# A written-out order of all engines, replaced by another, in a transformer block on one core

## The chip, the core and the metric

The kernel runs on one core of one Trainium2 chip. The metric is the device time of one execution in microseconds (us). A second number is the span, from the first to the last instruction of the core in a profiled execution. An engine is one of PE (TensorE, matrix products), DVE (VectorE), ACT (ScalarE), POOL (GpSimd), and SP (SyncE, which only issues transfers here). DMA stands for the transfers between the device's main memory and the on-chip memory.

## The reference

One block of a transformer, 2048 rows of 512 in fp32, one batch. The condition `c` gives six vectors by one product; attention and a feed-forward part follow, each behind a layer norm that two of the vectors scale and shift.

```python
mod = (_silu(c) @ w_mod).reshape(c.shape[0], 6, 1, -1)
sa, ca, ga, sb, cb, gb = (mod[:, i] for i in range(6))
h = _layernorm(x, axis=-1) * (1 + ca) + sa
x = x + ga * _A_ref(h, A_wq, A_wk, A_wv, A_wo, A_beta)
h = _layernorm(x, axis=-1) * (1 + cb) + sb
x = x + gb * _B_ref(h, B_w1, B_b1, B_w2, B_b2)
```

`_A_ref` has 32 heads of 16 and goes through the rows in 4 segments of 512. In each segment it takes causal softmax attention inside the segment, mixed by a gate with a read from a memory `M, z` that the earlier segments have filled (`num = phi(q) M`, `den = phi(q) z`); then the segment's keys and values are added to the memory. `_B_ref` is `relu(x @ w1 + b1)**2 @ w2 + b2` with 1792 hidden columns.

## The kernel before

The kernel has no loop that runs on the chip. Python builds a list of 3905 nodes; a node is a few instructions of one engine (`op("ACT", duration, fn, priority, after=..., get=..., put=...)`). `Plan.run` plays the nodes through a small model of the engines, hands out buffers in the order in which the model frees them, and the instructions are then emitted in the order that it found. Where the module constant `ORDER` lists an engine's nodes by number, that engine takes them in exactly that order. All five engines are listed in full, so `ORDER` is the order of each engine's queue; the model's durations decide only which buffer a node gets.

The work goes by row blocks of 512 (`s`, 0 to 3), in attention by units (`u = 4 s + cc`, a quarter of the heads each), with half units `qd`.

- **Start.** The six transfers of `w_mod`, `x`, `wq`, `wk`, `wv` are issued on SP. PE runs warm-up products (`bwarm`, nodes 8 to 77, line 536, two passes each) between its first real work. `ln_transposed` (line 621) turns one 128-row tile of the normed rows: PE transposes into `blnq` (nodes 105, 111, 117, 123 for the tiles 0 to 3 of block 0), ACT and DVE scale and shift (`lnf`, lines 611 and 613), ACT casts the high part into `HT` (line 618; nodes 108, 114, 120, 126), and DVE subtracts it to get the low part (line 618; nodes 109, 115, 121, 127; on POOL for later blocks). Every operand of an exact product is split so, into a high and a low part of the type fp32r, and a product takes three matmuls.
- **Weights.** `split_w` casts `wq`, `wk` (tile `WQK`) and `wv` (`WVO`) on ACT (line 695) and subtracts on POOL (line 699), by 128 columns: nodes 130 and 131 are the first columns of `wq`, 140 and 141 those of `wk`. The first QK products are the nodes 280 to 297 (lines 779 to 781): 280 to 283 and 290 to 293 are for the rows of the tiles 0 and 1. `clear` fills `ST` with zeros by DMA (nodes 158 to 160).
- **Attention.** For each unit: QK, split (`sg`, lines 821 and 823), twelve transfers that lay the heads out in `ST` (line 839), scores for the row maxima (`ba`, lines 894 and 899), scores again (`bpb`, line 1063), exp on ACT (`pt`, line 1080), the causal mask on POOL (line 1067), times V (`bpv`, line 1122). Meanwhile `make_w1` prepares `w1` in main memory (`w1d`) for the feed-forward part.
- **FFN.** For each row block, seven blocks of 256 hidden columns. `fetch_w1` brings one block's weights into one of two buffers (`w<-w1d`, line 1425; 3684 to 3687 are the blocks 3 to 6 of the last row block). Seven products of half blocks (`bh`, line 1475) are put together on DVE, squared, split (`rr`), and multiplied with `w2` into `bpf` (lines 1539 to 1541). When a row tile is done, DVE adds it to the rows (line 1550) and a store leaves on SP (line 1552): nodes 3122 to 3131 are the stores of row block 0, 3379 to 3388 of block 1, 3636 to 3645 of block 2, and 3893, 3896, 3899, 3902 of block 3 (3904, on ACT, is half of the last tile). Before that, the rows get the term `b2` on DVE (line 1545).

SP issues its transfers in the listed order: one that waits for its data holds up those behind it. The end of the SP list before:

```python
3681-3683 3636 3684-3685 3128 3379 3686 3125 3687
3902 3122 3645 3642 3899 3893 3896 3388 3382 3385 3639
```

Of the kernel before, what the change touches and what calls it, by code (L numbers as in the profile page):

```python
# [69 lines left out]
1160-1161 1259 1170 1497 1173 1498 1178 1401 1359 1182-1183 1407 1184 1256 1540 1275 1541 1250 1542 1278 1543 1186  # L70
1282 1545 1290 1546 1285 1547 1364 1262 1548 1373 1523-1524 1380 1367 1525 1388 1294-1296 1370 1298 1526 1391 1301
1528 1305 1376 1529-1531 1394 1308 1659-1660 1557 1661 1565 1662 1599 1313 1664-1665 1385 1602 1666-1667 1571 1397
1317 1605 1318-1319 1410 1794 1568 1795 1321 1578 1796 1413 1797 1562 2074 2079 1586 1799 1592 1800 1417 1801 1420
1574 1802 1425 1734 1692 1429 1583 1433 1430-1431 1436 1929-1930 1589 1931 1440 1932 1448 1452 1443 1934 1706 1935
1608 1936-1937 1611 1595 1453 1703 2084 1700 2089 1454 1697 1615 1713 1721 1618 1456 1623 1627 1718 1737 1628 1709
1631 1740 1638 1869 1634 1629 1724 1641 1827 1841 1646 1650 1727 1743 1872 1651-1652 1832 1746 2093 1750 1730 2094
1835 1753 2095 1848 1838 2096 1654 1758 1875 1762 1862 1766 1763-1764 1844 1773 2098 1769 2099 1776 2100 1856 1781
2101 2004 1962 1785-1787 2007 1859 2122 1853 1878 2123 1885 2124 1970 1865 2125 1888 1789 2127 1881 2128 1973 2129
1983 2130 2251 1997 2252 2198 1893 2253-2254 1976 1988 1897-1899 1967 1901 2256 1991 2257 1979 1908 2258 1916 2259
1994 2139-2140 2156 2141-2142 2170 1911 1904 2144-2146 2167 2000 2147 2177 2191 1920 2164 2013 1921-1922 2010 2161  # L80
2020 2375 2016 2376 2028 2188 2377 2173 2378 2023 1924 2380 2185 2381-2382 2301 2182 2383 2032-2034 2036 2306 2322
2499 2043 2500 2039 2501 2194 2502 2309 2051 2315 2504-2505 2280 2506 2046 2312 2507 2285 2055 2288 2201 2056-2057
2318 2204 2059 2208 2211 2291 2216 2220 2446 2224 2227 2221-2222 2231 2294 2234 2243 2641 2239 2404 2409 2244 2418
2297 2245 2644-2645 2651 2646-2647 2325 2332 2328 2654-2655 2247 2340 2335 2656 2661 2657 2415 2425 2344-2346 2412
2348 2355 2664-2665 2671 2666-2667 2421 2439 2528 2351 2674-2675 2358 2536 2363 2681 2676-2677 2430 2542 2436
2684-2687 2721 2367-2369 2449 2433 2724-2726 2691 2456 2533 2452 2727 2694-2695 2442 2371 2459 2549 2696 2731 2697
2762 2464 2539 2468-2470 2472 2563 2545 2734-2735 2701 2557 2479 2482 2736 2704-2705 2737 2560 2475 2487 2706 2741
2707 2554 2491-2493 2573 2580 2583 2744-2746 2566 2576 2495 2588 2747 2774 2711 2592-2594 2596 2603 2570 2599
2714-2715 2611 2606 2716 2770 2717 2751 2615-2617 2766 2754 2619 2755-2757 2791 2781 2811 2801 2794 2784 2804
2785-2786 2805 2787 2795 2806 2796-2797 2906 2903-2905 2814 2807 2815 2908 2907 2909 2816 2929 2926-2927 2817 2928  # L90
2930 2932 2931 3064 3068 3066-3067 2949 2952 2950-2951 3065 3070 2954 3071 2953 3069 3076 2955 2975 3134 3078 2973
2972 2974 3072 3082 3074 2976 3142 3083 2978 2977 2999 3080 2995-2998 3000 3138 3081 3087 3084-3085 3001 3086 3091
3018 3023 3088 3019 3092 3021 3020 3090 3022 3095 3146 3024 3089 3099 3041 3046 3042 3096 3093 3045 3043 3097 3044
3047 3094 3098 3391 3100 3104 3103 3102 3107-3108 3176 3106 3110 3101 3105 3178 3114 3174 3109 3175 3113 3177 3196
3179 3195 3111 3180 3115 3119 3200 3198 3197 3118 3199 3117 3399 3123 3112 3116 3201 3126 3218 3321 3129 3325 3120
3324 3217 3216 3395 3219 3328 3222 3322-3323 3238 3220 3327 3221 3237 3326 3333 3243 3339 3329 3337 3331 3239 3241
3240 3242 3335 3341 3343 3345 3403 3260 3258 3340 3264 3344 3338 3342 3259 3348 3262 3261 3347 3263 3346 3352 3351
3283 3279 3284 3281 3280 3356 3355 3282 3350 3349 3301-3302 3285 3353 3300 3354 3303 3357 3361 3305-3306 3358 3362
3304 3365 3359 3363 3431-3432 3660 3367 3360 3364 3434 3368 3372 3366 3433 3370 3435 3369 3437 3453 3652 3374 3373
3436 3380 3452 3376 3648 3458 3454 3371 3656 3375 3377 3455-3456 3383 3386 3457 3474 3473 3479 3478 3475-3477  # L100
3580-3581 3584 3579 3578 3590 3582 3494-3496 3585-3586 3497 3499 3498 3583 3500 3596 3519 3592 3515 3588 3516-3517
3594 3597 3518 3595 3521 3599 3601 3520 3605 3600 3598 3536-3537 3541 3602 3606 3604 3608-3609 3613 3540 3538-3539
3610 3603 3542 3612 3558 3607 3557 3611 3559 3614-3615 3560 3563 3619 3616 3620 3562 3561 3623 3617 3689 3688 3618
3691 3627 3690 3624 3621 3693 3628 3694 3625 3622 3692 3629 3626 3630 3711 3634 3710 3633 3631 3712 3709 3714 3643
3715 3713 3732 3730 3736 3632 3733 3637 3640 3835 3838 3731 3837 3842 3849 3841 3734 3836 3735 3847 3751 3754 3753
# [12 lines left out]
1068 1067 687 924 699 675 698 674 686 1071 783-784 199 934 936 932 929 935 931 933 930 1073-1074 780 706 779 704 707
206 714 713 941 721-722 1482 709-710 717 955 950 948-949 956 947 716 952 946 953 951 1000-1001 1195 209 809-810 801
# [277 lines left out]
def block_kernel(ctx, tc, x, wq, wk, wv, wo, beta, w1, b1, w2, b2, c, wmod, out):  # L397
# [71 lines left out]
    op = PL.op  # L469
    TL = {}  # L470
# [149 lines left out]
    def ln_transposed(s, t, src, dst, pool, sc, bi, pr, after, put, wait=(), low="DVE", kind="#D"):  # L620

        b = ("lnq", sc, s, t)
        f = ("lnf", sc, s, t)
        n = pe("F", 0.357, lambda: ln_turn(bank(b), src()), pr, after=after, get=[(kind, b)] + ([(pool, f)] if pool != "xr" else []),
               put=put)
# [5 lines left out]
        h = act(512, lambda: ln_split(dst(), t, TL[f], low)[0](), pr + 0.02, sbuf=True, after=[*af, *wait], put=[f])  # L631
# [965 lines left out]
```

## Time and profile before

| | us |
|---|---|
| three runs: median (lowest to highest) | 796.09 (795.66 to 796.46) |
| the profiled execution | 795.43 |
| its span | 793.7 |
| PE busy | 764.5 (96%) |
| DVE, ACT, POOL busy | 599.3, 441.7, 323.4 |

A row of a timeline has the start, the duration, the engine, the line, the operation, the tiles that it writes and reads, and in brackets the idle time before it and what ended that. SPq and ACTq are issues of transfers. A row of waits has who waited for whom, the time in all, how often, and the longest. A row of windows has the busy time of each engine in a stretch, with the number of instructions, then the granted PE clock (1.00 is full), the mean busy share of the DMA engines and GB/s. Matmul ends are modelled, so a busy PE isn't PE at its peak.

### The profile page before, as it was taken

The numbers are of one execution on the slowest core, as the hardware profiler recorded it, in microseconds if no ns is written. First come the engines' busy times: TensorE is split into PE (matmuls) and PEld (weight loads), VectorE is DVE, ScalarE is ACT, GpSimd is POOL, SyncE is SP. The second block draws the span as 40 slices with busy tenths as digits, with TensorE's granted clock in tenths as the row PEclk, the third lists the DMA queues.
The fourth block names the chain that finished last, engine by engine and source line by source line (L and its number), as shares of the span: only waits on it lengthen the run. The fifth ranks groups of instructions, "written<-read, shape, count | busy, mean of one in ns | idle before, by whom it ended". The sixth has DMA issues, their size and how long they took to land.

```text
span 793.7 us, 18015 instructions
## 1 busy us (share of the span) xinstructions
PE 764.5 (96%) x6649; PEld 606.7 (76%) x6649; DVE 599.3 (76%) x1591; ACT 441.7 (56%) x1001; POOL 323.4 (41%) x400
## 2 busy tenths in 40 slices
PE   9899999989999999999999999999999999999995
PEld 8777666765677656787576669898989889889984
DVE  5688758978789678989988789787866876476543
ACT  2568967789878898686865653556121321121110
POOL 4576674688777887545342252442002010000000
PEclk9999989999999999999999999999999999999998
DMA  9576856542644533435452275665543454544613
GB/s 313 138 195 171 246 181 196 160 135 94 192 128 133 169 94 96 131 86 159 130 141 81 82 252 199 213 239 199 186 169 116 180 204 181 186 165 160 233 53 145
DMA packets 59265, 129.65 MB, mean 163 GB/s; under 512 B 8613, under 2 KB 23977, under 8 KB 55594
## 3 DMA queue, kind: packets, MB, share of 16 engines
q1 hardware_dynamic: 59026, 128.37, 50.3%
q8 instruction: 53, 0.87, 0.5%
q14 instruction: 34, 0.28, 0.1%
q10 hardware_dynamic: 152, 0.13, 0.1%
HBM read 81.29 MB, written 20.19 MB: 128 GB/s over the span
## 4 chain that ended last, share of the span: by engine, by line
PE 61%; ACT 8%; DVE 4%; DMA 2%; SPq 1%; issue 1%; POOL 1%; ACTq 0%; DVEq 0%; POOLq 0%
PE bh L1475 16%; PE bpf L1540 6%; PE bpf L1539 6%; PE bpf L1541 6%; PE bpv L1122 5%; PE bqk L787 4%; PE bpb L1063 3%; PE ba L894 3%; ACT pt L1080 3%; PE bv L860 2%; PE bwop L1218 2%; PE bwop L1220 2%; PE bwop L1219 2%; ACT lnf L611 1%; SPq L839 1%
## 5 line engine op out<-in xcount | busy, mean ns | idle before, releaser
L899 DVE CUSTOM_DVE_ANT_0 ba<-ba,msk 128x512 f32<-128x512 f32 (+2 forms) x384 | 192.3, 533 | 36.9 <-PE ba L894 23.3
L1080 ACT ACTIVATE pt<-bpb 128x512 f32<-128x512 f32 x320 | 173.7, 619 | 22.4 <-PE bpb L1063 19.1
L1475 PEld LDWEIGHTS bh<-H2o,w 128*128 128x128 f32 x1176 | 153.9, 189 | 11.6 <-ACT h2raw L1281 1.4
L1475 PE MATMUL bh<-H2o,w 128*128 128x256 f32 x1176 | 157.8, 282 | 1.4 <-DVE h2raw L1283 0.8
L1067 POOL TENSOR_SCALAR_AFFINE_SELECT pt<-pt 128x512 f32<-128x512 f32 x128 | 79.6, 638 | 87.7 <-ACT pt L1080 65.0
L787 PE MATMUL bqk<-HT,WQK 64*128 64x512 f32 x720 | 104.4, 399 | 0.0
L1521 ACT CAST rr<-xx 128x512 fp32r<-128x512 f32 x56 | 34.4, 620 | 97.3 <-DVE xx L1511 60.2
L894 PE MATMUL ba<-ST 63*128 63x256 f32 (+2 forms) x512 | 79.7, 351 | 5.5 <-DMA ST<-sg 1.4
L1122 PE MATMUL bpv<-pt,VT 128*32 128x512 f32 (+3 forms) x1024 | 83.7, 448 | 0.7 <-POOL pt L1067 0.4
L1063 PE MATMUL bpb<-ST 64*128 64x256 f32 (+2 forms) x512 | 80.4, 352 | 2.2 <-ACT e L828 0.7
L787 PEld LDWEIGHTS bqk<-HT,WQK 64*128 64x128 f32 x720 | 73.3, 187 | 6.5
L894 PEld LDWEIGHTS ba<-ST 63*128 63x128 f32 x512 | 51.4, 186 | 31.2 <-ACT pt L1080 7.1
L1063 PEld LDWEIGHTS bpb<-ST 64*128 64x128 f32 x512 | 52.5, 188 | 21.1 <-ACT pt L1080 4.7
L1539 PE MATMUL bpf<-w,rr 128*128 128x512 f32 x160 | 63.5, 397 | 0.0
L1540 PE MATMUL bpf<-w,rr 128*128 128x512 f32 x160 | 63.0, 393 | 0.0
L1541 PE MATMUL bpf<-w,rr 128*128 128x512 f32 x160 | 62.5, 391 | 0.0
L860 PE MATMUL bv<-WVO,HT 64*128 64x512 f32 x384 | 54.9, 397 | 0.0
L899 DVE DVE_READ_ACCUMULATOR2_ANT mx<- 128x1 f32 x384 | 54.3, 141 | 0.0
L1122 PEld LDWEIGHTS bpv<-pt,VT 128*32 128x32 f32 x1024 | 27.3, 110 | 33.7 <-issue 25.5
L1523 DVE TENSOR_TENSOR rr<-xx,rr 128x512 fp32r<-128x512 f32 x56 | 40.0, 720 | 12.7 <-ACT rr L1521 12.6
L1501 ACT COPY p<-bh 128x256 f32<-128x256 f32 x28 | 10.4, 371 | 63.2 <-PE bh L1475 34.9
L1498 DVE SCALAR_TENSOR_TENSOR u<-bh,b1c,u 128x256 f32<-128x256 f32 x56 | 26.9, 480 | 24.3 <-PE bh L1475 23.2
(171 smaller groups left out, 1459.8 us busy)
## 6 DMA issues: line engine op xcount, KB each, us to landing
w<-w1d SPq DMA_DIRECT2D x28, 1792.0 KB
ST<-sg SPq DMA_DIRECT2D x192, 128.0 KB
w1d<-X1L SPq DMA_DIRECT2D x21, 512.0 KB
xt<-in_A_x SPq DMA_DIRECT2D x16, 256.0 KB
wm<-in_w_mod SPq DMA_DIRECT2D x16, 256.0 KB
xw<-in_A_x SPq DMA_DIRECT2D x16, 256.0 KB
X1L<-in_B_w SPq DMA_DIRECT2D x7, 512.0 KB
wr<-in_B_w SPq DMA_DIRECT2D x14, 256.0 KB
```

The costliest lines, as they stand in the source:

```text
L787: nc.tensor.matmul(bank(banks[w]), W3(w, k, x, cols.start, cols.stop)[r], HT[r, y, k], start=turn == k == i == 0, stop=turn == 1 and k == ...
L860: nc.tensor.matmul(bank(banks[t]), HT[r, x, k, (t2 + t) * P:(t2 + t + 1) * P], WVO[r, k, y], start=turn == k == i == 0, stop=turn == 1 and ...
L894: nc.tensor.matmul(dst[:, c0:c0 + n], ST[b:b + 63, 0, sl, qt * P:(qt + 1) * P], ST[b:b + 63, 1, sl, :n], start=True, stop=True)
L899: nc.vector.tensor_tensor_reduce(i, i, msk[:, 512 - n:], scale=1.0, scalar=-3e38, op0=ALU.add, op1=ALU.max, accum_out=o)
L1063: nc.tensor.matmul(dst, ST[b:b + 64, 1, sl, kb * P:(kb + 1) * P], ST[b:b + 64, 0, sl, q0:512], start=True, stop=True)
L1067: nc.gpsimd.affine_select(out=ap, in_=ap, pattern=[[0, ap.shape[1]], [1, P]], compare_op=ALU.is_ge, fill=0.0, base=0, channel_multiplier=-1)
L1080: ns = [op("ACT", 0.49, lambda j=j: nc.scalar.activation(buf("PPP"[n], pt)[:, i + j], bank(keys[j]), AF.Exp, scale=0.25), pr[slot] + 0.01 ...
L1122: nc.tensor.matmul(bank(o)[32 * hq:32 * hq + 32, q0:q0 + src.shape[1]], v[:, a:a + 32], src, start=start, stop=stop, tile_position=(0, 32 ...
L1475: nc.tensor.matmul(pb(i), A[:, x, kk], B[:, y, kk], start=kk == j == 0, stop=kk == 1 and j == 2)
L1539: nc.tensor.matmul(q, rh, wh, start=(i == 0), stop=False)
L1540: nc.tensor.matmul(q, rh, wl, start=False, stop=False)
L1541: nc.tensor.matmul(q, rl, wh, start=False, stop=(i == NF - 1))
```

## The change

All five lists of `ORDER` are replaced: the same nodes in another order. On PE 889 of 1315 nodes have another place, 212 by more than five; on ACT 742 of 945; on DVE 693 of 897; on POOL 238 of 342; on SP 331 of 403. The lists were searched for the mean end over six sets of durations, with the end of the stores counted. Beside that, the low part in `ln_transposed` is marked `lock=True`, by which the model lets it share one port with POOL's operations. The parts of the lists that the prediction speaks of:

```diff
 "PE", start
-... 3 28-40 86 94 111 41 88 42-45 96 46-51 123 52 105 53 117 54-77 280-281 290 282-284 291-292 ...
+... 3 27-37 105 38-41 111 42 86 94 43 88 96 44-47 123 48-52 117 53-72 290 73-77 280-281 291 282-284 292 ...
 "ACT", start
-1 4 87 95 112 130 124 106 118 140 126 108 120 114 150 152 142 ...
+1 4 87 95 130 140 112 124 106 114 108 126 118 120 150 142 144 ...
 "DVE", start
-2 98-99 110 101 100 89 122 97 104 113 116 125 107 119 127 109 121 115 151 ...
+2 98-99 101 104 110 100 122 89 97 113 116 125 107 119 115 109 127 121 151 ...
 "POOL", start
-102-103 141 131 143 157 133 153 155 ...
+102-103 141 131 143 133 157 155 153 ...
 "SP", start
-82 78 90 79 83-84 91 85 92-93 81 80 128 138-139 129 148-149 5 858 860-861 859 158 160 159 ...
+78-79 82 90 85 81 92 83 91 84 93 80 128 138-139 160 158 148 129 149 858-861 5 ... 161 159 ...
 "PE", around node 532 (modulation columns in attention)
-... 575-577 652 579 532 670 ...
+... 575-577 532 652 579 670 ...
 "ACT", around node 531 (its copy)
-... 896 898 657-658 902 905 531 899 ...
+... 896 898 902 899 531 657-658 905 ...
 "SP", the fills of unit 8 (1511 to 1522)
-... 1518 242 1516 1514 1513 1512 1265 1511 1522 1519-1521 246 245 1515 1517 1379 249 ...
+... 1515 1522 1517 1519 1521 242 1514 1265 1511 1516 1512 1518 1513 246 245 1379 249 1520 ...
 "PE", end
-... 3888 3886 3885 3889-3890 3894 3900 3887 3891 3897
+... 3877 3886 3883 3890 3887 3881 3885 3900 3889 3897 3891 3888 3894
 "SP", end
-3681-3683 3636 3684-3685 3128 3379 3686 3125 3687
-3902 3122 3645 3642 3899 3893 3896 3388 3382 3385 3639
+3681-3683 3385 3684 3388 3685 3645 3128 3382 3122 3379 3125 3686 3642 3636 3687 3131 3639
+3902 3899 3893 3896
@@ ln_transposed
-        l = op(low, 1.24 if low == "POOL" else 0.6, lambda: ln_split(...)[1](), pr + 0.03, after=[h], put=[f])
+        l = op(low, 1.24 if low == "POOL" else 0.6, lambda: ln_split(...)[1](), pr + 0.03, after=[h], put=[f], lock=True)
```

More of the change, by code (lines that the diff above doesn't have):

```diff
@@ new lines @@
+1331-1332 980 1333 1134 1334 992 1097 1137 1110 728 850 1118 1005 851-852 1121 1008 1012 1124 1015 854 1020 1471 1100
+1094 1476 1024 1028 1103 1115 1269 1486 1031 1025 1272 1106 1224 1232 1035 1038 1026 1238 1043 1047 1235 1140
+1048-1049 1127 1147 1490 1143 1229 1491 1051 1155 1492 1150 1493 1245 1159 1404 1253 1495 1241 1496 1163 1166
+1160-1161 1259 1170 1497 1173 1498 1178 1401 1359 1182-1183 1407 1184 1256 1540 1275 1541 1278 1542 1250 1543 1186
+1282 1545 1290 1546 1285 1364 1547 1262 1548 1373 1523 1380 1524 1367 1525 1388 1294-1296 1370 1298 1526 1391 1301
@@ new lines @@
+1835 1753 2095 1848 1838 2096 1654 1758 1875 1762 1862 1766 1763-1764 1856 1773 2098 1776 2099 1769 1844 2100 1781
+2101 2004 1962 1785-1787 1859 1878 2122 1853 2123 2007 1885 2124 1865 2125 1970 1888 1789 2127 1983 2128 1881 2129
+1973 2130 1997 2251-2252 1988 2253 1893 2198 2254 1976 1897 2010 1898-1899 1967 1901 2256 1908 2257 1916 1991 2258
+1979 2259 1994 2139 2156 2140-2142 1904 1911 2167 2144-2145 2170 2000 2146 2177 2191 2147 1920 2164 2013 1921-1922
+2188 2020 2375 2161 2376 2185 2377 2016 2378 1924 2023 2380-2381 2028 2182 2382 2173 2383 2301 2306 2032-2034 2036
@@ new lines @@
+2322 2499-2500 2043 2312 2501 2194 2502 2039 2309 2051 2504-2505 2315 2046 2506-2507 2280 2288 2055 2285 2201
+2056-2057 2318 2208 2059 2204 2211 2291 2216 2220 2224 2446 2227 2221-2222 2231 2234 2294 2641 2239 2243 2404 2418
+2297 2244-2245 2409 2644 2651 2645-2646 2325 2328 2332 2654 2647 2655 2335 2340 2415 2656 2661 2657 2425 2412
+2344-2346 2348 2355 2247 2664 2671 2665-2666 2439 2351 2421 2667 2674 2528 2536 2363 2675 2681 2676-2677 2542 2358
+2436 2684-2687 2721 2367-2369 2433 2449 2430 2724-2726 2691 2456 2533 2452 2727 2694-2695 2442 2371 2459 2549
@@ new lines @@
+2696-2697 2731 2464 2539 2563 2468-2470 2472 2545 2762 2734 2557 2479 2482 2735 2701 2736-2737 2475 2487 2560
+2704-2707 2741 2491-2493 2573 2580 2554 2583 2744-2745 2566 2576 2495 2588 2746 2711 2774 2747 2592-2594 2596 2603
+2599 2714-2715 2751 2606 2570 2611 2716-2717 2766 2615-2617 2770 2754 2619 2755-2757 2791 2811 2781 2801 2794-2795
+2784-2785 2796-2797 2786-2787 2903 2905 2904 2814-2815 2909 2804 2908 2906 2805 2816 2907 2806 2817 2932 2926 2807
+2927 2931 2928-2930 3065 3069 3064 3142 3138 2949 2951 2950 2954 2952-2953 3067 3066 3068 3071 2955 2972 2974 2973
@@ new lines @@
+3072 3074 2975 2977 3070 3078 3080-3081 2978 3085 2976 3083 2995 3001 2996 3076 2997 3087 2998 3084 3134 3146 3082
+3091 3089 3000 2999 3019 3086 3020 3018 3021 3088 3093 3024 3023 3090 3094-3095 3022 3044 3098 3092 3041-3042 3096
+3100 3099 3043 3102 3047 3046 3104 3045 3097 3101 3103 3107 3106 3105 3111 3108 3395 3110 3175 3174 3112 3109 3176
+3399 3177 3391 3115 3179-3180 3197 3178 3116 3114 3113 3195 3118 3126 3196 3403 3117 3119 3129 3123 3200 3199 3198
+3201 3323 3220 3219 3217 3324 3216 3120 3218 3221 3321 3222 3325 3328 3335 3322 3237 3239 3326 3238 3240 3329 3242
@@ new lines @@
+1894 1900 1902-1903 1909-1910 1918 1917 1980-1981 2260 2266 2262 2157-2158 2263 2143 1906 1905 1913 1912 2001-2002
+2179 2178 2151 2149 2152 2150 2155 2154 2015 2153 2014 2148 1923 2021-2022 277 2017 2379 2018 2025 2024 2029-2030
+2174-2175 2384 2390 2303 2302 2035 2386 2038 2037 2387 2044-2045 2196 2195 2503 2040 2052 2041 2053 2048 2047 2282
+2281 2202-2203 2058 2319 2637 2320 2210 2209 2206 2205 2213 2212 2633 2217 2508 2218 2226 2225 2514 2228-2229 2625
+2223 2232-2233 2236 2235 2642 2240-2241 2629 2298-2299 2406 2405 2510 2246 2511 2652 2329 2334 2327 2333 2330 2326
@@ new lines @@
+1003 991 1201 1207 988 987 961 960 1268 1267 979 985 984 982 981 1093 1099 1098 1138 1336 1342 729-730 1120 1119
+1122-1123 1126 1125 856 855 1102 1096 1101 1095 1104 1117 1105 1116 1114 1273 1233-1234 1240 1239 1237 1236 1228
+1230-1231 1052-1053 1254-1255 1249 1260-1261 2068-2069 1402 1500 1403 1408 2071 1258 1257 1506 2070 1252 1251
+1187-1188 1363 1366 1365 1374-1375 1368-1369 1390 1389 1371-1372 1392-1393 1384 2073 2078 1396 1395 1386 1567 1387
+1600 1566 1561 1601 1573 1572 1669 1675 1323 1322 1570 1569 1563-1564 1587-1588 1594 1593 1582 2088 1736 1735 1804
@@ new lines @@
+3570 3567 3676 3668 3572 3672 3569 3571 3575 3556 3678 3680 3696-3697 3574 3577 3699 3698 3700-3701 3703 3702
+3717-3718 3705 3720 3641 3722 3724 3719 3706 3635 3721 3726 3723 3727 3738 3708 3739 3638 3741 3740 3742 3744 3644
+3729 3748 3743 3745 3759-3760 3762 3761 3750 3764 3763 3766 3765 3780-3781 3747 3769 3783 3785 3787 3771 3782 3784
+3786 3790 3801 3768 3792 3802-3803 3805 3804 3807 3811 3789 3806 3808 3810 3822 3813 3823 3825 3827 3829 3831 3824
+3826 3828 3832 3834 3903 3901 3898 3892 3895
@@ L203 @@
[L203 to L206 removed]
+102-103 141 131 143 133 157 155 153 866 137 135 302 353 303 145 462 163 463 147 374 166 168-171 173 621 479 622 403
@@ L225 @@
+2879 3167-3173 3424-3430 3681-3683 3385 3684 3388 3685 3645 3128 3382 3122 3379 3125 3686 3642 3636 3687 3131 3639
+3902 3899 3893 3896
 """,
@@ L631, in ln_transposed @@
         h = act(512, lambda: ln_split(dst(), t, TL[f], low)[0](), pr + 0.02, sbuf=True, after=[*af, *wait], put=[f])
-        l = op(low, 1.24 if low == "POOL" else 0.6, lambda: ln_split(dst(), t, TL[f], low)[1](), pr + 0.03, after=[h], put=[f])
+        l = op(low, 1.24 if low == "POOL" else 0.6, lambda: ln_split(dst(), t, TL[f], low)[1](), pr + 0.03, after=[h], put=[f], lock=True)
         return [h, l]
```

258 lines of the change are left out of this document (105 added, 153 removed), and 14 rows, old and new, of the table ORDER.

## The prediction

> **What bounds the kernel now.** I read the page first: the busy shares, the row of granted clock, the transfers.
>
> ```profile
> span 793.7 us, 18015 instructions
> PE 764.5 (96%) x6649; PEld 606.7 (76%) x6649; DVE 599.3 (76%) x1591; ACT 441.7 (56%) x1001; POOL 323.4 (41%) x400
> PEclk9999989999999999999999999999999999999998
> w<-w1d SPq DMA_DIRECT2D x28, 1792.0 KB
> out<-X SPq DMA_DIRECT2D x12, 256.0 KB
> ```
>
> TensorE is busy 96% of the span and the change adds and removes no instruction, so nothing can come from its work. It can come only from time in which PE is idle or runs at a reduced clock. Second view: busy time by stage, with the edges that I chose (start of the dense matmuls, end of attention, end of the FFN).
>
> ```profile
> core 0: us, PE busy (x) PEld busy (x) DVE busy (x) ACT busy (x) POOL busy (x), PEclk, DMA share, GB/s
> 0.00:29.20 29.20, 23.93 (x190) 21.98 (x190) 17.48 (x32) 12.94 (x27) 13.55 (x33) 1.00 0.96 295
> 35.00:461.00 426.00, 414.00 (x4402) 293.91 (x4400) 352.89 (x1115) 333.79 (x786) 257.35 (x327) 0.98 0.48 141
> 461.00:785.00 324.00, 320.77 (x2026) 285.01 (x2024) 225.30 (x441) 94.66 (x188) 47.15 (x38) 1.00 0.50 180
> 785.00:793.70 8.70, 0.00 (x0) 0.00 (x0) 0.42 (x1) 0.00 (x0) 0.00 (x0) 0.65 0.79 294
> ```
>
> A 256 KB store is 0.262 MB. Three places hold what an order can move: the 29.2 us before the first dense matmul, 12.0 us of PE idle time in attention (with some half clock), and 8.7 us at the end with PE finished and DMA busy. In the FFN PE idles 3.2 us of 324.
>
> **Part 1: the stores at the end.** The third view is the timeline of the last 12 us, and the windows there.
>
> ```profile
> 719.09 12.14 SPq L1425 DMA_DIRECT2D w<-w1d  x2
> 731.28 0.90 SPq L1552 DMA_DIRECT2D out<-X  x2
> 738.66 0.33 SPq L1425 DMA_DIRECT2D w<-w1d  x1
> 782.69 2.73 DVE L1550 TENSOR_TENSOR X1L<-bpf,X1L 128x256 f32<-128x256 f32 x5 [2.19 <-PE bpf L1541]
> 783.15 0.39 ACTq L1552 DMA_DIRECT2D out<-X1L  x1
> 783.85 1.45 SPq L1552 DMA_DIRECT2D out<-X  x3
> 785.45 1.62 SPq L1552 DMA_DIRECT2D out<-X1L  x3
> 787.11 2.70 SPq L1552 DMA_DIRECT2D out<-X  x4
> 760.00:784.00 24.00, 24.00 (x127) 20.52 (x127) 11.67 (x24) 2.75 (x5) 0.00 (x0) 1.00 0.00 1
> 783.00:784.00 1.00, 1.00 (x6) 0.84 (x5) 1.00 (x3) 0.00 (x0) 0.00 (x0) 1.00 0.00 0
> 785.00:786.00 1.00, 0.00 (x0) 0.00 (x0) 0.42 (x1) 0.00 (x0) 0.00 (x0) 1.00 1.03 379
> 791.00:792.00 1.00, 0.00 (x0) 0.00 (x0) 0.00 (x0) 0.00 (x0) 0.00 (x0) 0.50 0.72 266
> ```
>
> Seven stores named out<-X, of earlier row blocks whose results are long done, leave after 783.85: three ahead of the last block's X1L stores and four behind them. DMA had moved nothing for 24 us; then it ran at 379 GB/s until about 791.7 (266 of 379 in the last window). From the last byte to the end of the span it is 2.0 us. The new SP order puts all seven between the last weight fetches (block 2 to block 6 of the last row block), and closes with 3902, 3899, 3893, 3896, all of the last block. What is late next: the last add ends at 782.69 + 2.73 = 785.42. Its store issues there; the first store (issued 783.15, no byte in 783 to 784) shows about 0.9 us to its first byte, and 0.262 MB at 0.379 MB/us take 0.7: last byte at 787.0. The 1.05 MB of the last block, begun at 784.0, would end at 786.8, so the last store decides. End 789.0 in place of 793.7: **gain 4.7 us**. Bounds: the last store of before shows 1.9 us from the end of its issue (789.81) to the last byte; with that the after lands at 787.7, a gain of 4.0; if the last rows of PE run a little earlier, 5.0.
>
> [...]
>
> The queue that they are moved past: behind fetch 4, out at 731.2, now go six stores instead of two. Issuing costs 0.45 us each (0.90 for two), done by 734, and fetch 5 leaves at 738.66 anyway. Their bytes are four stores more, 1.05 MB or 2.8 us, ahead of fetch 5, which needs 1.84 MB or 4.8 us. With two buffers a fetch goes out one block of PE work ahead of its use, 324/28 = 11.6 us; 0.9 + 2.8 + 4.8 leave 3.1 us. Cost nothing; were that cover gone, 0.7 us for each store.
>
> **Part 2: the start.** Fourth view: what each engine does before 33 us.
>
> ```profile
> PE bqk L780 <- DVE HT L618: 3.4, 1, 3.4
> L618 DVE TENSOR_TENSOR HT<-lnf,HT x4: 680/1553/1757, 23.9 to 27.4; 128x512 fp32r<-128x512 f32 x4
> 23.86 5.31 DVE L618 TENSOR_TENSOR HT<-lnf,HT 128x512 fp32r<-128x512 f32 x4 [1.96 <-ACT HT L618]
> 23.39 1.28 POOL L699 TENSOR_TENSOR WQK<-w,WQK 128x512 fp32r<-128x512 f32 x1 [8.97 <-DMA xt<-in_A_x]
> 24.62 1.73 POOL L699 TENSOR_TENSOR WQK<-X1L,WQK 128x512 fp32r<-128x512 f32 x1
> 31.98 2.56 POOL L699 TENSOR_TENSOR WVO<-w,WVO 128x512 fp32r<-128x512 f32 x2
> 17.25 0.81 ACT L611 ACTIVATE lnf<-blnq,modc 128x128 f32<-128x128 f32 x2 [2.89 <-DVE modc L586]
> 22.70 0.61 ACT L695 CAST WQK<-w 128x512 fp32r<-128x512 f32 x1
> 20.05 5.52 PE L536 MATMUL bwarm<-ident 128*128 128x128 f32 x48
> 29.23 0.38 PE L780 MATMUL bqk<-HT,WQK 128*128 128x256 f32 x1 [3.40 <-DVE HT L618]
> 39.40 1.57 PE L860 MATMUL bv<-WVO,HT 64*128 64x512 f32 x12
> 29.80:33.20 3.40, 3.40 (x18) 3.40 (x17) 2.63 (x5) 0.00 (x0) 3.40 (x3) 0.50 0.28 66
> 33.20:36.60 3.40, 3.40 (x31) 3.27 (x29) 0.41 (x1) 0.59 (x1) 1.34 (x2) 1.00 0.00 0
> ```
>
> PE fills the time with warm-up matmuls until 25.57, starts the first QK product, and waits 3.40 us for the low parts of HT. Those four subtractions on DVE take 680 ns at best and mostly twice that, beside POOL's subtractions of the weights, which began at 23.39 because ACT casts the wk columns only at 22.70. Then the clock is at half for 3.4 us: 18 matmuls where the next window has 31, so 13/31 of 3.4, 1.4 us, are lost.
>
> The new orders touch this chain four times. ACT casts both weights (130, 140) right after the two copies of the modulation, in the 2.89 us in which it waited: 2 x 0.61 fit, if the loads are there. POOL's first two subtractions can then run some 6 us earlier, and DVE is alone. ACT casts HT of a row tile as soon as it is scaled, and the low parts go 115, 109, 127, 121: tiles 1 and 0 first, which is all that the first half of QK needs. On PE, 290 and five warm-ups are put ahead of 280. DVE's four at 0.68 then take 2.7 instead of 5.31; even from the same start, 23.86, the first two would end at 25.2. PE itself is late next: 20 warm-ups after the last transposes instead of 24 (48 passes took 5.52, so 40 take 4.6) put 290 at 24.65; 0.35 for it and 1.15 for five warm-ups put 280 at 26.15, against 29.23. That is 3.1 us, and the half clock goes too, 1.4: **gain 4.5 us**. It must also not be given back at V: V starts at 39.40, POOL's last part of WVO ends at 34.54, 4.9 us of cover, and POOL itself moves ahead. Bounds: nothing (two fills of ST with zeros now go ahead of the rest of wq and wv on the SP queue, in a stretch with DMA at 0.96) to 5.6 (if the transposes move ahead too). I take the middle-high value because the wait is one wait with one cause.
>
> **Part 3: attention and FFN.** Order changes nearly everywhere, mostly by under ten places, with 181 switches of PE's mode before and 179 after. Followed closely, one stall:
>
> ```profile
> 103.30 0.65 ACT L568 COPY t<-bmod 128x512 f32<-128x512 f32 x1
> 104.00 1.08 PE L584 MATMUL bmodc<-selc,t 128*128 128x1 f32 x8 [0.97 <-ACT t L568]
> PE ba L894 <- DMA ST<-sg: 1.4, 1, 1.4
> 101.48:104.89 3.41, 2.44 (x32) 1.61 (x24) 1.39 (x3) 2.53 (x7) 3.29 (x4) 1.00 0.97 295
> 104.89:111.72 6.83, 6.44 (x66) 4.70 (x65) 3.71 (x14) 5.18 (x12) 3.37 (x4) 0.50 0.42 144
> ```
>
> ACT's copy (531) has two operations fewer ahead of it there, about 1 us, so the 0.97 us should mostly go: I take **1.0 us** and nothing for the clock behind it. For the rest I assume that new stalls replace old ones. Bounds: 5 us gained, under half of the 12.0 idle plus the half clock, to 7 lost. The FFN is at nothing: PE hides the moved DVE adds (L1545), and the last products stand no closer to the matmuls that need them. The flag lock=True changes only the planner's arithmetic and, through it, buffer numbers: nothing.
>
> **The sum.** 4.7 + 4.5 + 1.0 = 10.2 us off the profiled execution's own 795.43 (span 793.7 and 1.7 around it) gives 785.2; the median of the runs is 796.09, 0.66 above, so 785.9.
>
> **Rivals.** (a) Attention gives back 4 to 7 us through new stalls while both ends gain: 790 to 793. For it: the order is scrambled everywhere; against: the stalls of before are small and spread. (b) The start does not gain, since the fills delay the weights, or the low parts still meet POOL: 785.9 + 4.5, 790.4. (c) Slower, by half clock in attention. The place is the fills of ST ahead of the scores (the wait of 1.4 us on ST<-sg): the new SP order mixes the twelve fills of a unit otherwise and puts more transfers among them. Price: 1.4 for the wait and 1.4 for one half-clock window behind it, 2.8. To be slower by 1.6 it must cost 11.8 us, so it decides from five such new stalls, one for every third of the 16 units: 14 us, 799.9. Against it: DMA share is 0.48 in attention. [...] (d) The edits cancel: within 1.6 us of 796.
>
> **How the numbers follow.** Forecast (781 to 789) 0.62; (a) 0.15; (b) 0.12; (d) 0.03; (c) 0.08. About 0.2%, 1.6 us, is what a measurement can tell from no change. Faster: 0.62 + 0.15 + 0.12 = 0.89. Low end: 5.0 + 5.6 + 5.0 off 796.1 is 780.5; high end: 794.0 takes in (a) and (b) and leaves (c) and (d) out.
>
> **What would show it.** Right: no out<-X store after the last row block's, the last byte within 2 us of the last add, PE's first long wait gone and the clock at full from 23 to 40 us, DVE's L618 near 0.7 us each. Wrong: L618 still above 1.3 us with POOL beside it, first QK product after 28 us, more than three stretches at half clock in attention, or PE waiting on the fetched weights near 750 us.

## The result and the profile after

| | before | after |
|---|---|---|
| median of the runs on one chip (lowest to highest), us | 796.22 (795.66 to 796.46), 4 runs | 778.70 (777.84 to 779.99), 4 runs |
| ratio, with its 95% interval | | 0.9782 (0.9765 to 0.9799) |
| profiled execution and its span, us | 795.43, 793.7 | 778.83, 777.1 |

The change takes 17.5 us off where 10.2 were forecast. The sign is as forecast, the time lies below the range (780.5 to 794.0). The lines of the page of after that answer to the first ones of before:

```profile
span 777.1 us, 18036 instructions
PE 761.9 (98%) x6649; PEld 603.3 (78%) x6649; DVE 591.7 (76%) x1591; ACT 443.3 (57%) x1001; POOL 324.8 (42%) x400
PEclk9999999999999999998899999999999999999999
```

PE is busy 2.6 us less in all, so most of the 16.6 us of span were time in which it stood still. Where: the windows of before, cut at the first dense QK product, the first product of the FFN and PE's end, then those of after, cut at the same events.

```profile
0.00:29.23 29.23, 23.93 (x190) 21.98 (x190) 17.51 (x32) 12.97 (x27) 13.58 (x33) 1.00 0.96 295
29.23:469.31 440.08, 426.76 (x4503) 304.03 (x4503) 363.02 (x1136) 336.77 (x793) 267.88 (x336) 0.98 0.49 143
469.31:784.69 315.38, 313.77 (x1957) 280.65 (x1957) 218.07 (x424) 92.00 (x182) 41.93 (x33) 1.00 0.49 176
784.69:793.70 9.01, 0.00 (x1) 0.00 (x0) 0.73 (x2) 0.00 (x0) 0.00 (x0) 0.66 0.80 296
```

```profile
0.00:25.96 25.96, 24.05 (x192) 22.36 (x193) 15.43 (x32) 11.26 (x24) 12.25 (x32) 1.00 0.95 316
25.96:458.89 432.93, 424.29 (x4504) 300.27 (x4502) 359.15 (x1135) 340.16 (x798) 269.79 (x336) 0.98 0.51 146
458.89:772.88 313.99, 313.51 (x1957) 280.63 (x1957) 216.41 (x424) 91.85 (x180) 42.77 (x33) 1.00 0.51 183
772.88:777.10 4.22, 0.00 (x1) 0.00 (x0) 0.69 (x1) 0.00 (x0) 0.00 (x0) 1.00 0.39 146
```

The first number behind the edges is the length. Start −3.3, attention −7.2, FFN −1.4, end −4.8. In attention PE's idle time (length less PE busy) goes from 13.3 to 8.6 us. The cut puts the half clock behind the first wait of before into attention, so about 1.4 of the 7.2 belong to the prediction's Part 2.

The timeline of after at its end and in its first 26 us:

```profile
769.95 0.38 ACTq L1552 DMA_DIRECT2D out<-X1L  x1
770.28 3.69 SPq L1552 DMA_DIRECT2D out<-X1L  x4
772.92 0.69 DVE L1550 TENSOR_TENSOR X1L<-bpf,X1L 128x512 f32<-128x512 f32 x1 [0.67 <-PE bpf L1541]
...
17.03 1.27 POOL L699 TENSOR_TENSOR WQK<-w,WQK 128x512 fp32r<-128x512 f32 x1 [2.98 <-ACT WQK L695]
18.26 1.58 POOL L699 TENSOR_TENSOR WQK<-X1L,WQK 128x512 fp32r<-128x512 f32 x1
21.81 1.89 DVE L618 TENSOR_TENSOR HT<-lnf,HT 128x512 fp32r<-128x512 f32 x3
23.88 0.69 DVE L618 TENSOR_TENSOR HT<-lnf,HT 128x512 fp32r<-128x512 f32 x1 [0.18 <-ACT HT L618]
24.50 0.36 PE L779 MATMUL bqk<-HT,WQK 128*128 128x256 f32 x1
24.93 1.27 PE L536 MATMUL bwarm<-ident 128*128 128x128 f32 x10
25.96 0.36 PE L779 MATMUL bqk<-HT,WQK 128*128 128x256 f32 x1
```

No store of an X tile is left behind the last block's. POOL is done with the first weights at 19.8, before the low parts begin; those take 0.63 to 0.69 us each; 290 runs at 24.50 and 280 at 25.96 with no wait. (The forecast had 24.65 and 26.15.) The granted clock of after is full until 272.6 us.

A third view, worked out from the two traces, is the lead: the start of the n-th matmul of before less that of the n-th of another kernel, at some times of before. It goes by count, so where the orders differ it compares two different products. For e9 and e15 see below.

| us in before | 44 | 102 | 118 | 187 | 223 | 313 | 385 | 457 | 613 | 774 |
|---|---|---|---|---|---|---|---|---|---|---|
| lead of after | 5.0 | 5.9 | 9.1 | 10.3 | 12.7 | 13.3 | 10.8 | 9.5 | 11.5 | 12.5 |
| lead of e9 | 4.7 | 4.9 | 8.1 | 9.5 | 12.2 | 12.3 | 12.2 | 12.2 | 12.3 | 12.3 |
| lead of e15 | −0.5 | −0.6 | 0.8 | 0.2 | 2.3 | 3.0 | 2.3 | 1.2 | 2.6 | 2.1 |

After the start, two steps stand out: 3.2 us between 102 and 118, and 2.4 between 187 and 223. (The fall of 2.5 between 313 and 385 goes with after's own half clock from 364.8 to 375.0, see the last section.) The place of the first step was in the forecast with 1.0. The runs had to say whether these steps come from the order.

### The profile page after: what moved, and what is told of

The parts are those of the page before. It is cut to its first block, busy times and chain, and to the rows that moved or that the text cites. A ratio compares the mean times of both kernels' runs of the same rounds, so it can differ in the third digit from the quotient of the medians.

```text
span 777.1 us, 18036 instructions
## 1 busy us (share of the span) xinstructions
PE 761.9 (98%) x6649; PEld 603.3 (78%) x6649; DVE 591.7 (76%) x1591; ACT 443.3 (57%) x1001; POOL 324.8 (42%) x400
## 4 chain that ended last, share of the span: by engine, by line
PE 59%; DVE 4%; ACT 1%; issue 1%; DVEq 0%; ACTq 0%
PE bh L1475 18%; PE bpf L1540 7%; PE bpf L1539 7%; PE bpf L1541 7%; PE bpv L1122 4%; PE bpb L1063 3%; PE bqk L787 2%; PE ba L894 2%; PE bwop L1218 2%; PE bwop L1220 2%; PE bwop L1219 2%; PE bv L860 1%; DVE ba L899 1%; PE blnq L605 1%; PE bmr L987 1%; PE bwot L1245 1%
## 5 line engine op out<-in xcount | busy, mean ns | idle before, releaser
L899 DVE CUSTOM_DVE_ANT_0 ba<-ba,msk 128x512 f32<-128x512 f32 (+2 forms) x384 | 192.4, 533 | 32.7 <-PE ba L894 19.8
L1080 ACT ACTIVATE pt<-bpb 128x512 f32<-128x512 f32 x320 | 171.6, 611 | 22.4 <-PE bpb L1063 19.9
L787 PE MATMUL bqk<-HT,WQK 64*128 64x512 f32 x720 | 102.5, 396 | 0.2 <-ACT phi L830 0.2
L787 PEld LDWEIGHTS bqk<-HT,WQK 64*128 64x128 f32 x720 | 69.1, 185 | 9.6 <-ACT phi L830 0.6
L1314 POOL TENSOR_TENSOR tt<-h2raw 128x512 f32<-128x512 f32 x8 | 10.9, 1372 | 89.2 <-DVE H2o L1330 56.1
L938 DVE TENSOR_REDUCE mx<-ac 128x4 f32<-128x1024 f32 x32 | 38.9, 1215 | 7.5 <-POOL ac L935 7.5
```

The costliest lines, as they stand in the source:

```text
L787: nc.tensor.matmul(bank(banks[w]), W3(w, k, x, cols.start, cols.stop)[r], HT[r, y, k], start=turn == k == i == 0, stop=turn == 1 and k == ...
L899: nc.vector.tensor_tensor_reduce(i, i, msk[:, 512 - n:], scale=1.0, scalar=-3e38, op0=ALU.add, op1=ALU.max, accum_out=o)
L1080: ns = [op("ACT", 0.49, lambda j=j: nc.scalar.activation(buf("PPP"[n], pt)[:, i + j], bank(keys[j]), AF.Exp, scale=0.25), pr[slot] + 0.01 ...
```

## The experiments

Each kernel is the kernel before with a part of the new order, unless said otherwise. Nodes are named by number; a set of nodes is put, in the places that the set holds before, into the order in which the change has them. A gain is (1 − ratio) times the median of the kernel before in the same session (795.31, 796.70, 794.58 and 795.47 us), in brackets the 95% interval. The ratios are as recorded; the quotient of two medians differs from them by up to 0.23%, which is within the intervals.

**The stores at the end (e1).**

```diff
 "SP", end
-3424-3427 3131 3428-3430 3681-3683 3636 3684-3685 3128 3379 3686 3125 3687 3902 3122 3645 3642 3899 3893 3896 3388 3382 3385 3639
+3424-3430 3681-3683 3385 3684 3388 3685 3645 3128 3382 3122 3379 3125 3686 3642 3636 3687 3131 3639 3902 3896 3893 3899
```

> The kernel before, with the SP list alone changed at its end: the seven old stores stand among the last weight fetches as in the change, and the last four stores follow the adds as this kernel makes them. If the end is bound by the bytes of those stores: 4.5 to 5 us less (791.4), last byte within 2 us of the last add, the rest of the trace unmoved. If the stores delay the fetches behind them: less than 3 us gained, and PE waits appear between 710 and 760 us.

Median 790.76, ratio 0.995 (0.993 to 0.997): 4.0 us (2.4 to 5.6). From its timeline:

```profile
782.18 2.73 DVE L1550 TENSOR_TENSOR X1L<-bpf,X1L 128x256 f32<-128x256 f32 x5 [2.19 <-PE bpf L1541]
782.97 2.31 SPq L1552 DMA_DIRECT2D out<-X1L  x4
```

The last add ends at 784.91 and the span at 788.5, 3.6 us later; the prediction's sum has the same 3.6 (785.42 to 789.0), after has 3.5 (773.61 to 777.1). Part 1 is shown, and by this edit alone.

**The start, first attempt (e2).** The start's nodes on all engines. One place on SP is unlike the change: the load 161 (line 729) stands ahead of the transfers 305 to 315 of the first unit into `ST`; in both kernels compared it stands behind them.

```diff
 "SP", start
-... 158 160 159 305-306 312 304 310-311 307-308 313 315 314 309 161 ...
+... 160 158 148 5 129 149 858-861 161 305-306 312 304 310-311 307-308 313 315 314 309 159 ...
```

> The kernel before, with the nodes of the start (warm-ups, modulation, norm and split of block 0, first weights, first QK) in the order of the change on all engines, everything else as before. If the start's gain carries through: 4.5 to 5 us less (791.4), the first QK product at about 26 us, the four low parts of HT near 0.7 us each, no half clock at 30 us. If attention behind it was not bound by PE, part of it is lost again by 100 us: 1 to 3 us less.

Median 797.60, ratio 1.0044 (1.0016 to 1.0072): slower by 3.5 us. Its timeline, then a window:

```profile
41.91 0.38 SPq L729 DMA_DIRECT2D X1L<-in_B_w  x1
42.38 5.87 SPq L839 DMA_DIRECT2D ST<-sg  x9
47.36 0.58 PE L894 MATMUL ba<-ST 63*128 63x256 f32 x2 [6.56 <-DMA ST<-sg]
```

```profile
44.90:51.80 6.90, 3.85 (x18) 2.67 (x18) 1.96 (x9) 1.36 (x3) 1.21 (x2) 0.51 0.81 242
```

The load waits until 41.91 for the place that it fills (POOL's last subtraction out of that tile ends at 41.89), and nine transfers into `ST` wait behind it on the queue. PE stands 6.56 us, to 47.36; the clock is 0.51 from 44.90 to 51.80, and PE is busy for 3.85 of these 6.9 us. The gain of the start (a lead of 4.4 at 44 us) is given back and more. It is the mechanism of rival (c), with its price paid at one place; it says nothing against the start, so the start was tried again.

**The start, second attempt (e5).** The same, with 5, 304 to 315, 161 and 159 as in the change. The SP list against that of e2:

```diff
-... 160 158 148 5 129 149 858-861 161 305-306 312 ...
+... 160 158 148 129 149 858-861 5 305 304 312 306 311 310 308 315 307 313 309 314 161 159 ...
```

> The start once more, as in e2_start, but with the twelve fills of unit 0 inside the exchanged part of the SP list, so that the load 161 (which waits until POOL has split all of wq) stands behind them, as in the change, and not ahead. If that load held up the fills in e2_start: the wait of 6.6 us before the first scores goes, and 4 to 5 us less than before (791). If the first scores wait for something else that comes no earlier: still a wait of 3 us or more at 41 us, and no gain.

Median 792.20, ratio 0.9935 (0.991 to 0.996): 5.2 us (3.2 to 7.2), where Part 2 had 4.5.

**What of the start does it (e10, e11).** e10 moves two casts on ACT and nothing else; e11 leaves the casts and puts the tiles 1 and 0 first on ACT and DVE.

```diff
 e10, "ACT"
-95 112 130 124 106 118 140 126
+95 130 140 112 124 106 118 126
 e11, "ACT" and "DVE"
-106 118 140 126 108 120 114       119 127 109 121 115
+106 114 140 108 126 118 120       119 115 109 127 121
```

> The kernel before with two nodes moved, 130 and 140 on ACT (the first casts of wq and wk) right behind the second copy of the modulation. If POOL's subtractions are what slows the low parts of HT: POOL starts L699 near 17 us, the four L618 of DVE take about 0.7 us each, the first QK products go at 26.5 us, the half clock at 30 us goes, 3.5 to 4.5 us less. If they are slow for another reason (operands, the ACT casts): L618 stays above 1.3 us and the time within 1 us of before.

> The kernel before with the scaling, casts and low parts of block 0 in the order of the change on ACT and DVE (tiles 1 and 0 first), the weights' casts left where they were, so that POOL still works beside DVE. If the order of the tiles alone were enough: the first QK product with a low part at 26.5 us and 3 to 4 us less. If the shared time with POOL decides: L618 stays at 1.3 us or more, and at most 1.5 us less.

e10: median 788.41, ratio 0.9912 (0.988 to 0.9944), 7.0 us (4.4 to 9.5). e11: median 790.40, ratio 0.9937 (0.9908 to 0.9966), 5.0 us (2.7 to 7.3). The timelines, e10 first:

```profile
16.20 1.53 POOL L699 TENSOR_TENSOR WQK<-w,WQK 128x512 fp32r<-128x512 f32 x1 [1.11 <-ACT WQK L695]
17.70 1.27 POOL L699 TENSOR_TENSOR WQK<-X1L,WQK 128x512 fp32r<-128x512 f32 x1
22.65 2.48 DVE L618 TENSOR_TENSOR HT<-lnf,HT 128x512 fp32r<-128x512 f32 x4
26.23 0.37 PE L779 MATMUL bqk<-HT,WQK 128*128 128x256 f32 x1
```

```profile
22.02 1.27 POOL L699 TENSOR_TENSOR WQK<-w,WQK 128x512 fp32r<-128x512 f32 x1 [7.30 <-ACT WQK L695]
22.24 5.61 DVE L618 TENSOR_TENSOR HT<-lnf,HT 128x512 fp32r<-128x512 f32 x4
25.75 0.36 PE L779 MATMUL bqk<-HT,WQK 128*128 128x256 f32 x1
25.95 0.28 PE L780 MATMUL bqk<-HT,WQK 128*128 128x256 f32 x1
```

With POOL done first, the four subtractions take 0.62 us each (2.48 for four). With POOL beside them they take 1.40 (5.61), and QK still starts at 25.75 without a wait, since the two that it needs come first. Within the intervals each edit alone brings what the whole start brings (e5): the cure was there twice, and the two don't add. Between these two runs the four differ by a factor of 2.3 (5.61 to 2.48 us); why, no trace shows.

**The stall at 104 us, the edit that the prediction named (e3).**

```diff
 "ACT"
-898 657 658 902 905 531 899
+898 902 899 531 657 658 905
 "PE"
-652 579 532
+532 652 579
```

> The kernel before, with nine nodes moved: on ACT the copy 531 goes ahead of the two copies of the score maxima and of phi, on PE the product 532 that needs it goes ahead of two others, as in the change. If the wait of 0.97 us at 104 us is what brings the two windows of half clock behind it (6.83 us, half of which is 3.4): 4 to 5 us less (791.7), and no half clock between 100 and 115 us. If the half clock has another cause: 1 us less, half clock still there.

Median 795.30, ratio 1.0009 (0.9981 to 1.0036): nothing. The wait of 0.97 us on line 584 is down to 0.38, and another stands 3 us behind it (timeline, then the window):

```profile
106.74 0.90 PE L1063 MATMUL bpb<-ST 64*128 64x256 f32 x3 [0.90 <-DVE modc L586]
```

```profile
106.60:110.00 3.40, 3.26 (x17) 3.26 (x18) 1.85 (x10) 1.77 (x4) 3.13 (x3) 0.50 0.36 108
```

**The whole stretch (e6), then by engines (e13, e14).** All nodes that run between about 95 and 126 us, in the new order: 116 nodes change their place, 24 of them on PE. e6 takes all engines, e13 PE alone, e14 the other four.

```diff
 "PE", part
-... 530 575-577 652 579 532 670 586 1056-1057 589 680 538 ...
+... 530 680 575-577 532 652 579 670 1056 586 1057 589 538 ...
 "SP", part (908 to 919 fill ST)
-... 536 655 916 191 544 543 545 914 911 542 909 915 908 195 910 913 918 194 919 912 917 ...
+... 535 915 446 655 191 543 544 542 545 918 912 917 909 919 916 194 910 195 908 914 911 913 ...
```

> The kernel before, with all nodes of about 95 to 126 us in the order of the change on all engines, nothing else. If the stall at 103 us and the half clock behind it are mended by the orders there: no PE gap over 0.5 us between 98 and 118 us, no half clock there, 3 to 4 us less (791.5). If the change escapes it only because it comes there 5 us earlier or with other waits behind it: within 1.5 us of before.

> The kernel before with PE's order alone of the stretch from about 95 to 126 us (55 nodes; a filler product 1056 ahead of 586, 680 and 532 earlier); the other four engines as before. If PE's order is what mends the waits of that stretch, most of the 4 us that all five engines' order brought there comes back: about 792, no PE gap over 0.4 us between 95 and 126 us. If it is the SP order of the fills of ST, or ACT's, this stays within 1.5 us of before, with a gap of 0.9 us or more near 104 us.

> The counterpart: the kernel before with the order of ACT, DVE, POOL and SP of the same stretch, PE as before. If PE's order alone mends the stretch: within 1.5 us of before, with a wait near 104 us. If the other engines' order does it: about 792 and no gap over 0.4 us there. If both are needed, both kernels stay above 793.

e6: median 791.33, ratio 0.9946 (0.9923 to 0.9968), 4.3 us (2.5 to 6.1). e13: median 794.23, ratio 1.0004 (0.9981 to 1.0027). e14: median 794.50, ratio 1.0003 (0.9975 to 1.003). The window of that stretch for before, then for e6:

```profile
95.00:126.00 31.00, 29.64 (x325) 20.22 (x323) 21.03 (x76) 20.51 (x45) 17.44 (x21) 0.89 0.71 225
```

```profile
95.00:126.00 31.00, 31.00 (x360) 21.52 (x358) 23.97 (x82) 24.10 (x53) 19.35 (x23) 1.00 0.81 250
```

Before: 1.36 us idle and a mean clock of 0.89; e6: no idle time, full clock, 35 matmuls more in the same 31 us. Each is one run. With one half of the order, a wait stands near 100 us, a little ahead of the old place; first e13, then e14:

```profile
99.76 1.06 PE L564 MATMUL bmod<-wm,cs 128*32 128x512 f32 x8 [0.86 <-PE ba L894]
```

```profile
100.87 1.06 PE L564 MATMUL bmod<-wm,cs 128*32 128x512 f32 x8 [0.85 <-DVE mx L899]
```

The windows of the stretch, e13, then e14:

```profile
95.00:126.00 31.00, 30.03 (x344) 21.04 (x342) 22.01 (x80) 22.68 (x50) 18.75 (x22) 1.00 0.76 236
95.00:126.00 31.00, 29.70 (x338) 19.68 (x336) 21.83 (x77) 21.61 (x48) 17.99 (x22) 1.00 0.73 228
```

Neither PE's order nor the others' alone brings e6's gain: their intervals (−2.1 to 1.5 and −2.4 to 2.0 us) lie apart from e6's. It takes both, which was the third of the cases written down for e14. This rests on the medians. In the two profiled runs PE idled 1.0 and 1.3 us here, without half clock, with 344 and 338 matmuls between before's 325 and e6's 360, so they alone would suggest a part of the gain for each half.

**Parts put together (e4, e7, e9, e8).**

```diff
 e4: before + e1 + e2 + e3
 e7: before + all nodes up to about 126 us in the new order (e5, e6 and what lies between)
 e9: e7 + e1
 e8: the change itself
```

> The three partial changes together: end, start, and the nine nodes. If they are independent and the copy carries the half clock: 13 to 14.5 us less (782.3), and some 3.5 us of the change's gain is left to the rest of attention. If the gain of attention is spread over many places: 10 to 11 us less (785.6), 7 left.

> The kernel before, with all nodes up to about 126 us in the order of the change, the old order from there on (old stores at the end too). If start and the stretch to 126 us make most of the gain: a lead of 8 to 10 us at 120 us, held to the end: 786.5. If the later order of before cannot hold the lead, because it waits there for other engines: 2 to 5 us less only.

> e7_to120 and e1_tail together: the order of the change up to about 126 us and for the seven old stores, the order of before for the 640 us between. If the change's gain lies in these two places: 15 to 17 us less than before (780 to 782). If the new order of the rest of attention and of the FFN is worth several us by itself: 786 or more.

> The change itself, unaltered, beside the others on their chip: 778 to 780 if its gain is a property of the order; 783 or more if the first comparison caught lucky phases of the clock windows.

e4: 791.45, ratio 0.9951 (0.9927 to 0.9975), 3.9 us (2.0 to 5.8), with e2's wait of 6.6 us in it. That is e1's gain, though e1, e2 and e3 taken alone add up to −0.2. e7: 786.25, ratio 0.9874 (0.9844 to 0.9904), 10.0 us. e9: 780.41, ratio 0.9799 (0.9762 to 0.9837), 16.0 us (13.0 to 18.9). e8: 778.99, ratio 0.9784 (0.9751 to 0.9817), 17.2 us (14.6 to 19.8). With the new order up to about 126 us and the stores, nearly all of the change is there. (None of the partial kernels has the flag `lock=True`, so its effect, through the buffer numbers, was not measured alone; e9 comes near the whole without it.)

**The order behind 126 us alone (e15).** The complement of e9: start, first stretch and end as before.

```diff
 before + all nodes behind about 126 us in the new order, without the stores at the end
```

> The kernel before with the new order of everything behind 126 us, in attention and the feed-forward part, but with the start, the stretch up to 126 us and the stores at the end as before. If the rest of the order brings nothing (the prediction's assumption that new stalls replace old ones): 794 to 798. If it has a share of its own, half clock taken out of the later units: 791 to 793, with PE gaining on before by 3 us or more between 170 and 330 us.

Median 794.71, ratio 0.9994 (0.9968 to 1.002): 0.5 us (−1.6 to 2.5). So the second step of the lead isn't the new order's: e9, which has the old order there, shows it as well (9.5 to 12.2). It goes with one stretch at half clock at 217 us in the profiled run of before (0.50 from 217.50 to 220.90); the mean clock of that run is 0.985, that of e9's 0.997. e1, which has the orders of before there, gains 2.2 us at that place. The first step is in part of the same kind: e15, with the order of before there, gains 1.4 (−0.6 to 0.8). Before's run had 6.83 us at half clock behind the stall, and 1.4 us is what the prediction put on 3.4 of them.

**A version that goes on (e12).** After, with the last ten warm-up nodes (68 to 77) taken out, which do no part of the result, and the load 2067 behind the fills of its unit.

```diff
-pe("F", 0.22, lambda: nc.tensor.matmul(bank(wk_)[:, :P], ident, ident, ...), 50.0,
+pe("F", 0.22, (lambda: None) if i >= 60 else lambda: nc.tensor.matmul(...), 50.0,
```

> The change with the last ten warm-ups left out (they do no part of the result) and the load 2067 moved behind the fills of unit 7. QK's operands are there at 23.1 us, and PE reaches it at 24.5 only because of warm-ups: dense matmuls from 23.5, 2 us earlier than the change if nothing else is late (777), and the wait of 1.3 us at 205 us shorter by 0.6. If V's weights or the first fills of ST are then late: the lead is gone by 50 us, 778 to 780.

Median 778.43, ratio to before 0.9789 (0.9749 to 0.9829), beside 0.9784 for e8 in another session: not to be told apart from the change. The first QK product (290) starts at 23.38 instead of 24.50, and 280 follows at 23.82 instead of 25.96. In the profiled runs, with the same matmuls compared, PE is 2.2 us ahead of after at 30 us and 2.9 at 110; two waits on ACT, of 1.18 us at 165 and 1.22 at 208, take most of that, and 0.4 is left at 320. At the end it is 2.2 again; after's run was at half clock from 364.8 to 375.0 us, and its mean clock is 0.991 beside 0.995 in e12's.

## Why the prediction was wrong in size

**Part 1, 4.7 forecast: right.** e1 gave 4.0 (2.4 to 5.6), the traces 4.8 between PE's end and the end of the span. Seven stores among the fetches cost PE nothing, as said: e9's lead is the same at 613 and 774 us.

**Part 2, 4.5 forecast: right in time, only half right in cause.** e5 gave 5.2 (3.2 to 7.2). POOL beside DVE went with longer low parts (1.40 us each in e11, 0.62 in e10), and the first QK product came within 0.2 us of the forecast. But "one wait with one cause" was wrong: the order of the tiles alone removes the wait with POOL still beside (e11). The bound of 5.6 was passed by e10's median gain, within its interval.

**Part 3, 1.0 forecast: the step that failed.** It reads "ACT's copy (531) has two operations fewer ahead of it there, about 1 us, so the 0.97 us should mostly go: I take 1.0 us and nothing for the clock behind it". Both halves fell. The named edit alone brings nothing (e3), as the wait goes to the next consumer. The stretch as a whole brings 4.3 (2.5 to 6.1, e6). Rows of before held that size: two waits, the 0.97 and the 0.39 in this row of its timeline,

```profile
105.48 0.99 PE L894 MATMUL ba<-ST 63*128 63x256 f32 x4 [0.39 <-ACT phi L830]
```

and behind them 6.83 us at half clock, two windows at the 1.4 us that Part 2 had put on one: 0.97 + 0.39 + 2.8 = 4.2. In e1, with the old order there, one window (0.50 from 106.40 to 109.80) stood behind the stall, which makes it 2.8. Half clock was priced at the start and left at nothing 75 us later.

**"New stalls replace old ones" in the rest: right** for what lies behind 126 us (e15, 0.5 us). With 2.8 to 4.2 in Part 3 the sum is 12.0 to 13.4 and not 10.2, and the time 784.1 to 782.7, inside the range; the 4.0 to 5.4 us from there to 778.7 belong to the next paragraph. Part 3's bound failed too: between the two traces attention and the FFN give 7.1 us (5.7 and 1.4), where it allowed 5, while both ends stay within theirs. These are single runs, so some of the 7.1 may be theirs and not the order's.

**What stays open.** The parts measured alone add up to 4.0 + 5.2 + 4.3 + 0.5 = 14.0; the whole gave 17.2 beside one set of runs and 17.5 beside another. The intervals of the five numbers, taken together, allow 3.2 (the root of the sum of squares of their half widths, 1.6, 2.0, 1.8, 2.1 and 2.7, is 4.6), so it may be chance; that the parts help one another isn't shown, nor excluded. (e4 likewise is 4.1 above its parts, where the intervals allow 4.0.) The order between the start and 95 us was not run alone; e7 is 0.5 above e5 and e6 together. Which pairs of nodes in the 95 to 126 us stretch must move together wasn't found out either.

**Rivals.** (a) fell, attention gave more; (b) fell with e5; (d) fell. (c) didn't happen in the change, but e2 shows its mechanism at work for one transfer out of place.

## What to carry to other kernels

Price a stall with the half clock behind it, everywhere or nowhere: two waits of 1.4 us together had one or two windows behind them here, 2.8 to 4.2 us in all. When an order is said to remove a wait, ask who waits next within the following microseconds; here a single moved operation handed the wait on, and the stretch mended only with PE and the other engines together. A transfer that must wait for its place goes behind the transfers that PE needs on that queue: in e2 nine stood behind one that waited until 41.91, and PE idled 6.56 us.

## What the runs showed of the hardware

**The places and lengths of the half clock in these traces.** While PE works, before was at half clock for 3.41 us from 29.80, 6.83 from 104.89, 3.41 from 217.53 and 3.41 from 285.80; these starts are 22, 33 and 20 times 3.41 us apart. e1 has the same orders up to about 700 us. It was at half clock from 106.4, 280.4 and 376.0 us, which is 51 and 28 times 3.41 us apart, and 106.4 is 1.5 us behind before's 104.89. Before was at half clock from 104.89 to 111.72 and in the first two windows here, e1 in the three behind them (the last three numbers of a row are the clock, the DMA share and GB/s):

```profile
217.50:220.90 3.40, 3.40 (x52) 1.49 (x48) 1.29 (x2) 2.90 (x6) 1.80 (x2) 0.50 0.40 118
285.80:289.20 3.40, 3.24 (x28) 1.63 (x28) 2.36 (x10) 2.63 (x7) 2.12 (x4) 0.50 0.16 40
```

```profile
106.40:109.80 3.40, 3.40 (x19) 2.72 (x19) 1.74 (x8) 2.23 (x5) 2.54 (x3) 0.50 0.19 42
280.40:287.20 6.80, 6.71 (x49) 3.93 (x53) 4.01 (x15) 5.00 (x11) 5.51 (x7) 0.50 0.33 97
376.00:382.80 6.80, 6.80 (x44) 3.35 (x47) 5.60 (x15) 5.38 (x12) 3.46 (x4) 0.50 0.15 48
```

The same stall near 104 us had 6.83 us of half clock behind it in one run and 3.4 in the other, and at 376 us e1 alone is at half clock (before has 1.00 from 368 to 389). Two runs of one kernel differ as well: from 51.30 to 54.70 us the clock is 0.50 in e8's run and 1.00 in after's. Ahead of the half clock PE was not idle throughout: it was busy 2.44 of 3.41 us ahead of before's at 104.89, and 3.10 of 3.40 ahead of after's at 364.80 (the first two of the windows below). In the third PE idles 1.3 us of 4.0, and the clock is full in it and behind it (1.00 from 208 to 212). So in these rows PE's idle time alone doesn't tell where the half clock comes; what sets it off was not shown.

```profile
361.40:364.80 3.40, 3.10 (x27) 1.84 (x25) 3.26 (x11) 3.38 (x10) 0.29 (x1) 1.00 0.84 264
364.80:375.00 10.20, 10.10 (x69) 5.60 (x68) 6.72 (x15) 7.14 (x15) 4.98 (x6) 0.50 0.34 96
204.00:208.00 4.00, 2.71 (x47) 1.49 (x47) 2.73 (x9) 2.72 (x7) 3.69 (x6) 1.00 0.64 167
```

**The times of one kernel go with its mean clock.** The kernel before ran from 790.92 to 801.94 us over the sessions; its time goes with the mean granted clock of the run (correlation −0.68 to −0.83 in four sets of 18 to 31 runs). In these sets the line through the runs has 5.3 to 6.6 us for 0.01 of clock. One window of 3.41 us at half clock lowers the mean by 0.5 × 3.41 / 795 = 0.0021; by these lines that is, as an estimate, 1.1 to 1.4 us; the prediction's 13/31 of a window gave 1.4. A single profile of a kernel thus carries some us that belong to its run and not to its order: the 2.4 us at 187 to 223 above are an example.
